# Attention scores by full-height matmuls over block-diagonally spread queries, four heads per matmul, in a fused adaLN + sliding-window attention + gMLP kernel

## The chip, the cores and the metric

The kernel runs on one core of a Trainium2 chip. The metric is the device time of one execution, in microseconds (us). The kernel before had a median of 351.53 us over three runs (351.22 to 391.38). All five engines of the core take part: TensorE (called PE in the profile, its weight loads PEld), VectorE (DVE), ScalarE (ACT), GpSimd (POOL) and SyncE (SP), which here only issues DMAs.

The clock that is granted to TensorE differs between runs of the same kernel, and every run reports its mean. In this study the kernel before ran in 343.8 to 346.9 us at a clock of 0.985, in 345.4 to 346.7 at 0.970, in 350 to 354 at 0.949 to 0.956, in about 356 at 0.937, once in 359 at 0.924, and in 388 to 392 at 0.816. The run report calls a run slow when it is over 1.5% above the fastest run of the same kernel and the same call, and "fast runs" below are the others.

## The reference, cut to what matters

```python
# S = 2048 tokens, D = 448, H = 16 heads of Dh = 28, window W = 256, Fh = 896
mod = silu(c) @ w_mod                     # six rows of D: sa, ca, ga, sb, cb, gb
h = layernorm(x) * (1 + ca) + sa
q, k, v = split_heads(h @ wqkv)
scores = (q @ k.T) * Dh ** -0.5           # key i visible to query t if 0 <= t - i < 256
x = x + ga * ((softmax(mask(scores)) @ v) @ wo)
h = layernorm(x) * (1 + cb) + sb
z = gelu(h @ w_in);  z1 = z[..., :Fh];  z2 = layernorm(z[..., Fh:])
g = w_sp @ z2 + b_sp                      # w_sp: 2048 x 2048, mixes tokens
x = x + gb * ((z1 * g) @ w_out)
```

The window makes every tile of 128 queries see at most three blocks of 128 keys: its own (masked above the diagonal), the one before (not masked), and the one before that (masked the other way).

## The kernel before: the parts that the change and the argument touch

The kernel is written as a list of operations with dependencies, priorities and estimated costs. A list scheduler in Python runs once, before compilation; it simulates the five engines with those costs and fixes **the order of the instructions on each engine**. On the chip each engine then executes its own list strictly in order and waits on semaphores. So an estimate in the source (the `1000` in `dma=(131072, 1000)` is the latency in ns that the scheduler assumes for a DMA) never slows the chip by itself; it decides where in an engine's list the consumer stands.

The queries and keys are stored transposed and padded: four heads of 32 rows in 128 partitions. A score matmul takes one head, hence 32 rows of the array, and 128 columns. One exp covers two heads and up to three key blocks (768 columns).

```python
# scores: one matmul per head and key block, 32 rows high
for bi in reversed(range(nb)):
    if on_pe and bi == nmask - 1:                  # last three tiles: mask by matmul
        for hi in range(2):
            mm(e, ps[:, ten.slot + hi, 0:nmask*128], ident[:], maskn[:, 256-nmask*128:256], True, False)
    for hi, h in enumerate(heads):
        hh = h % 4
        mm(e, ps[:, ten.slot + hi, bi*128:(bi+1)*128],
           QKT[32*hh:32*hh+32, 4 + hg, kb*128:(kb+1)*128],
           QKT[32*hh:32*hh+32, hg, j*128:(j+1)*128], ..., tile_position=(32*hh, 0))
# exp (ACT), masks of 128x256 (POOL, except in the last three tiles), P @ V: 29 columns per head (28 + a column of ones)
...
# projections: D = 448 in four chunks of rows; the fourth is only 64 rows high
KC = ((0, 128), (1, 128), (2, 128), (3, 64))
mm(e, ps[:, ten.slot, 0:w], WQK[0:kw, kc, 4*g:4*g+4, :], hT[0:kw, kc, c0:c1], kc == 0, kc == 3)
...
# a tile's attention output: transposed by DMA (SyncE), then multiplied with wo
t1 = P.op("oT%d" % j, pr, [("sp", 1260, lambda e: e.dma_start_transpose(out=oT[...], in_=o_sb[...]))],
          [nrm, t_opad], alloc=oTt, table="tr", dma=(131072, 1000), uses=[ot])
...
# the spatial weights: 32 transposing DMAs, also on SyncE, in the background of the attention
wsp_op[(si, hf)] = P.op(..., [("sp", 1300, fn)], deps, table="wsp", dma=(390000, 1500))
```

## Time and profile before

| stage (profile of 343.6 us) | from | to | length |
|---|---|---|---|
| start, up to the first projection matmul (`ps<-hT,WQK`) | 0 | 17.4 | 17.4 |
| projections and attention | 17.4 | 170.3 | 152.9 |
| MLP (from the first matmul on `hT` and `w_in_sb`) and last stores | 170.3 | 343.6 | 173.3 |

The profiled run took 345.4 us at a clock of 0.970, so the time is the span plus 1.8 us. The first three fences are the kernel before. From its page: the busy share of TensorE in 40 slices of 8.6 us (in tenths, 9 is 90% or more), the granted clock in the same slices, the chain of waits that ended last, and some groups of instructions (busy us in all, mean ns of one, then idle time before them and what ended it).

```profile
span 343.6 us, 6679 instructions
...
PE   0799999999999999999999999999999999999995
...
PEclk9999999999999999995589999999999999999999
...
PE 91%; DMA 2%; DVE 2%; POOL 2%; ACT 1%; issue 0%; DVEq 0%; ACTq 0%
...
L681 ACT ACTIVATE PT<-ps 128x768 bf16<-128x768 f32 (+2 forms) x128 | 96.7, 770 | 37.1 <-PE ps L453 33.4
...
L453 PE MATMUL ps<-QKT 32*128 32x128 bf16 x720 | 46.2, 225 | 1.0 <-ACT PT L681 0.9
...
L692 POOL TENSOR_SCALAR_AFFINE_SELECT PT<-PT 128x256 bf16<-128x256 bf16 x104 | 43.2, 416 | 7.0 <-ACT PT L681 6.8
...
L453 PE MATMUL ps<-wo_sb,oT 128*128 128x448 bf16 x64 | 21.9, 382 | 0.2 <-DMA oT<-o_sb 0.2
```

TensorE is the bound: it is on 91% of the chain and the score group waited 1.0 us in all. But "busy" does not say what it is busy with. Matmuls are pipelined and overlap in the records (the sum of busy times counts an overlap once per group), so a mean of 225 ns is not the cost of a matmul. The cost is the step from one end to the next. The timeline of TensorE gives ends as start plus length (columns: start, length, engine, line, operation, tile and form as rows*columns, count):

```profile
101.25 0.30 PE L453 MATMUL ps<-Vaug,PT 128*128 128x29 bf16 x6
101.40 0.35 PE L453 MATMUL ps<-wqkv_sb,hT 128*128 128x448 bf16 x1
101.68 0.34 PE L453 MATMUL ps<-QKT 32*128 32x128 bf16 x6
101.95 0.36 PE L453 MATMUL ps<-wqkv_sb,hT 64*128 64x448 bf16 x1
102.24 0.31 PE L453 MATMUL ps<-Vaug,PT 128*128 128x29 bf16 x6
102.41 0.35 PE L453 MATMUL ps<-wo_sb,oT 128*128 128x448 bf16 x1
102.69 0.34 PE L453 MATMUL ps<-QKT 32*128 32x128 bf16 x6
```

The ends are 101.55, 101.75, 102.02, 102.31, 102.55, 102.76, 103.03. Where the height stays at 128 rows, the 448-column matmul ends 0.20 or 0.21 us later. Where the height changes, everything costs about 0.1 us more: the 64-row 448-column matmul takes 0.29 us, the six score matmuls 0.27 us (over the trace their ends come in pairs of two row groups, about 54 ns from pair to pair; three such steps would be 0.16), and the six 29-column matmuls after a 64-row one 0.24 us (6 x 25 ns would be 0.15). Over the whole trace, a 512-column matmul ends 216 ns after its predecessor when both are 128 rows high, and 322 ns after a 32-row one. From 17.3 to 140 us I count 328 such changes. The elapsed 122.8 us are 86.6 us of streaming, 34.4 us for 328 changes at 105 ns, and 1.8 us of rest. (The rest is what remains when every change is counted at 105 ns, so it is an estimate.)

The 216 ns agree with the Trainium skill, "TensorE: Matmul & The Clock Gate", section "Wait — 56ns, not 53.3ns?", which measures, at full clock, N/2.4 GHz plus about 2.5 ns from one back-to-back matmul to the next, 215.7 ns for N = 512.

The table by windows shows the second loss. Columns: window, length, busy time and count of PE, PEld, DVE, ACT, POOL, granted clock, DMA share, GB/s:

```profile
150.00:160.00 10.00, 9.54 (x108) 4.56 (x104) 2.35 (x8) 5.83 (x8) 0.55 (x1) 0.67 0.52 107
160.00:170.00 10.00, 9.87 (x94) 4.07 (x92) 2.38 (x7) 5.07 (x7) 0.55 (x1) 0.50 0.14 26
```

In the last tiles of the attention, where masks are matmuls, the granted clock falls to 0.67 and 0.50.

### The profile page before, as it was taken

What the parts mean: (1) busy time and instruction counts of PE and PEld (TensorE: products, weight loads), DVE (VectorE), ACT (ScalarE), POOL (GpSimd) and SP (SyncE); (2) the same over time, 40 slices, a digit from 0 to 9 for tenths busy, and PEclk for the clock granted to TensorE, in tenths of its full rate; (3) what the DMA queues carried; (4) which work ended last, traced back from release to release, by engine and by line L of the source; (5) the groups of instructions that cost most, each with busy time, mean ns of one, the idle gap of its engine ahead of it and who ended that gap; (6) DMA issues with size and microseconds to landing.
All of it is one profiled execution on the core that took longest, in us unless ns stands there. A gap on an engine that the chain in (4) does not pass through costs nothing.

```text
span 343.6 us, 6679 instructions
## 1 busy us (share of the span) xinstructions
PE 327.6 (95%) x2728; PEld 160.0 (47%) x2728; DVE 172.8 (50%) x402; ACT 143.2 (42%) x198; POOL 100.9 (29%) x247
## 2 busy tenths in 40 slices
PE   0799999999999999999999999999999999999995
PEld 0524554445555555544444444444444444444442
DVE  1895468786566555332157787123243233233333
ACT  0347667678788777675555566600000000000000
POOL 5123447789878788100012212000000000000000
PEclk9999999999999999995589999999999999999999
DMA  6997488998212120673010000000010001001001
GB/s 194 333 359 181 99 126 164 142 162 148 46 34 33 34 48 19 128 150 62 17 31 15 2 2 0 2 0 0 2 53 0 2 0 53 2 0 53 2 0 53
DMA packets 60062, 23.64 MB, mean 69 GB/s; under 512 B 52224, under 2 KB 58560, under 8 KB 60032
## 3 DMA queue, kind: packets, MB, share of 16 engines
q1 hardware_dynamic: 59552, 23.21, 30.8%
q8 instruction: 22, 0.36, 0.4%
q10 hardware_dynamic: 480, 0.00, 0.1%
q14 instruction: 8, 0.07, 0.1%
HBM read 8.78 MB, written 1.84 MB: 31 GB/s over the span
## 4 chain that ended last, share of the span: by engine, by line
PE 91%; DMA 2%; DVE 2%; POOL 2%; ACT 1%; issue 0%; DVEq 0%; ACTq 0%
PE ps L453 91%; DMA cT_sb<-in_c_dram 2%; ACT PT L681 1%; POOL PT L692 1%; POOL rs_all L516 1%; POOL PT L690 1%; DVE WQK L576 0%; ACT L445 0%; DVE fin L864 0%; DVE st_all L520 0%; DVE hT L568 0%; ACT hT L564 0%; DVE Vaug L626 0%; DVE sc_rep L447 0%; DVEq L873 0%
## 5 line engine op out<-in xcount | busy, mean ns | idle before, releaser
L681 ACT ACTIVATE PT<-ps 128x768 bf16<-128x768 f32 (+2 forms) x128 | 96.7, 770 | 37.1 <-PE ps L453 33.4
L453 PE MATMUL ps<-w_spA,z_73 128*128 128x512 bf16 x336 | 77.1, 379 | 0.0
L842 DVE TENSOR_TENSOR tmpg<-ps,bsp_bc 128x512 bf16<-128x512 f32 x28 | 19.4, 692 | 72.1 <-PE ps L453 72.1
L453 PEld LDWEIGHTS ps<-w_spA,z_73 128*128 128x128 bf16 x336 | 32.9, 98 | 39.4
L516 POOL TENSOR_TENSOR rs_all<-ve_all,neghalf 128x1 f32<-128x1 f32 (+2 forms) x40 | 23.8, 601 | 87.7 <-DVE ve_all L514 87.7
L453 PE MATMUL ps<-QKT 32*128 32x128 bf16 x720 | 46.2, 225 | 1.0 <-ACT PT L681 0.9
L453 PE MATMUL ps<-hT,WQK 128*128 128x512 bf16 (+3 forms) x160 | 45.4, 341 | 0.1
L692 POOL TENSOR_SCALAR_AFFINE_SELECT PT<-PT 128x256 bf16<-128x256 bf16 x104 | 43.2, 416 | 7.0 <-ACT PT L681 6.8
L690 POOL TENSOR_SCALAR_AFFINE_SELECT PT<-PT 128x256 bf16<-128x256 bf16 x88 | 36.3, 413 | 20.1 <-ACT PT L681 18.5
L453 PEld LDWEIGHTS ps<-Vaug,PT 128*128 128x128 bf16 x720 | 29.4, 97 | 14.8 <-issue 5.6
L453 PE MATMUL ps<-Vaug,PT 128*128 128x29 bf16 x720 | 35.5, 178 | 0.1
L453 PEld LDWEIGHTS ps<-QKT 32*128 32x128 bf16 x720 | 21.0, 93 | 26.3 <-PE ps L453 13.8
L453 PE MATMUL ps<-w_spB,z_73 128*128 128x512 bf16 x112 | 28.7, 379 | 0.0
L453 PE MATMUL ps<-w_in_sb,hT 128*128 128x448 bf16 (+1 forms) x128 | 28.4, 366 | 0.0
L453 PE MATMUL ps<-hT,w_in_sb 128*128 128x512 bf16 x112 | 27.0, 380 | 0.0
L820 ACT ACTIVATE z1T<-ps 128x512 bf16<-128x512 f32 x28 | 16.6, 598 | 17.4 <-PE ps L453 17.4
L520 DVE BATCH_NORM_STATS2 st_all<-z2raw 128x6 f32<-128x448 bf16 x32 | 19.5, 622 | 8.2 <-ACT z2raw L800 8.2
L520 DVE BATCH_NORM_STATS2 st_all<-x_sb 128x6 f32<-128x448 bf16 x32 | 19.0, 609 | 6.1 <-DMA x_sb<-in_A_x_dram 5.8
L453 PE MATMUL ps<-wo_sb,oT 128*128 128x448 bf16 x64 | 21.9, 382 | 0.2 <-DMA oT<-o_sb 0.2
L453 PE MATMUL ps<-w_out_sb,z1T 128*128 128x448 bf16 x112 | 21.8, 352 | 0.0
L453 PEld LDWEIGHTS ps<-hT,WQK 128*128 128x128 bf16 (+1 forms) x160 | 13.3, 95 | 16.0 <-issue 7.1
L606 DVE CAST QKT<-ps 128x256 bf16<-128x256 f32 (+1 forms) x28 | 14.8, 534 | 11.3 <-PE ps L453 11.3
(67 smaller groups left out, 270.5 us busy)
## 6 DMA issues: line engine op xcount, KB each, us to landing
x_sb<-in_A_x_dram SPq DMA_DIRECT2D x4, 448.0 KB, 8.5
out_dram<-fin SPq DMA_DIRECT2D x16, 112.0 KB, 1.7
w_in_sb<-in_B_w_in_dram SPq DMA_DIRECT2D x1, 1344.0 KB, 11.6
wqkv_sb<-in_A_wqkv_dram SPq DMA_DIRECT2D x1, 1008.0 KB, 9.1
wmod_sb<-in_w_mod_dram SPq DMA_DIRECT2D x1, 1008.0 KB, 9.4
w_out_sb<-in_B_w_out_dram SPq DMA_DIRECT2D x1, 784.0 KB, 13.1
wmod_sb<-in_w_mod_dram SPq DMA_DIRECT2D x1, 672.0 KB, 6.9
bsp_bc<-in_B_b_sp_dram SPq DMA_DIRECT2D x1, 512.0 KB, 13.7
```

Source lines behind the costliest of these rows:

```text
L453: return e.matmul(out_, lhsT=lhsT, rhs=rhs, start=st, stop=sp, **kw)
L516: return P.op(name + "rs", prio, [("pool", 500 + 130 * (t1 - t0 - 1), lambda e: e.tensor_tensor(rs_all[:, slot, t0:t1], ve_all[:, slot, t0 ...
L520: st = [P.op("%sst%d" % (name, i), prio, [("dve", dve_ns(D, base=145), lambda e, i=i, s_=s_: e.bn_stats(st_all[:, slot, t, i, :], s_()))], ...
L606: return e.tensor_copy(QKT[:, g, c0:c1], ps[:, ten.slot, 0:w])
L681: return e.activation(ptv(pt)[:, :, 0:nb, :], ps[:, ten.slot:ten.slot + 2, 0:nb * 128].rearrange("p h (b q) -> p h b q", q=128), ACT.Exp, ...
L690: e.affine_select(out=v[:, :, 0, :], in_=v[:, :, 0, :], pattern=[[0, 2], [-1, 128]], compare_op=ALU.is_gt, fill=0.0, base=0, channel_multi ...
L692: return e.affine_select(out=v[:, :, nmask - 1, :], in_=v[:, :, nmask - 1, :], pattern=[[0, 2], [1, 128]], compare_op=ALU.is_ge, fill=0.0, ...
L820: z1_op[(ft, tb)] = P.op("z1g%d_%d" % (tb, ft), pr, [("act", act_ns(512), lambda e, tb=tb, ft=ft, ten=ten: e.activation(z1T[:, ft, tb * 51 ...
L842: a = P.op("ga%d_%d" % (tb, ft), pr, [("dve", 692, lambda e, tb=tb, ten=ten, tg=tg: e.tensor_tensor(tmpg[:, tg.slot, :], ps[:, ten.slot, : ...
```

## The change: its intent, and the diff

The intent is to keep the array at full height. Queries are spread block-diagonally: a buffer of 128 partitions x (4 heads x 128 queries) holds head hh only in its own 32 partitions and zeros elsewhere. One matmul of 128 rows and 512 columns then gives the scores of four heads at once, against the 128-row key tile. SyncE makes the spread by four DMAs per pair of tiles, into two buffers that one GpSimd memset has zeroed. An exp now covers 1024 columns, and GpSimd makes all masks, 512 columns each. The fourth chunk of the projections becomes 65 rows (the 65th is a bias row, because the modulation is now folded into the weights) and that of the output projection is padded to 128. From the second block on, layer-norm outputs are transposed by DMA instead of by matmul. The conditioning vector is loaded as a row. The last spatial weights go to a third buffer.

The diff holds more than this list: sixteen warm-up matmuls on the identity at the start, new pacing constants for the scheduler, another order of the score units, and a rule that lets the spatial-weight transposes out only from the fourth tile on, some 2.5 per tile.

```diff
-    QKT, qkt_off, qkt_end = alloc("QKT", [128, 8, S], BF16)
+    KT, kt_off, _ = alloc("KT", [128, 4, S], BF16)
+    NQB = 2
+    QB_sb, _, _ = alloc("QB_sb", [128, NQB, 4, 4, 256], BF16)
+    qst, _, q_end = alloc("qst", [128, 2, 4, 512], BF16)
...
+    t_qb0 = pool1("qb0", -59.4, 4000, lambda e: e.memset(QB_sb[:], 0.0))
...
+    qb_m, t_bq = bias_row("bq", -43.5, 0, wqkv_sb, 0, t_sA + t_wqkv, WQK[64:65, 3, 0:16, 0:DH])
...   # WQK and wqkv scaled by the modulation, on DVE, POOL or ACT
+                hT_op[t] = P.op("hT%d" % t, pr + 0.2, [("sp", 1260, lambda e, t=t, ten=ten: e.dma_start_transpose(
+                    out=hT[:, t, :, :], in_=xn[:, ten.slot, :]))], [xn_op[t], t_xpad], table="tr", dma=(131072, 1000), uses=[ten])
...
+                def fn(e, hh=hh, pair=pair, tb=tb, off=off):
+                    return e.dma_start(QB_sb[32 * hh:32 * hh + 32, qb_ten[pair].slot, :, hh, :],
+                                       qst[32 * hh:32 * hh + 32, qst_ten[tb].slot, :, off:off + 256])
+                qb_op[(pair, hh)] = P.op("qb%d_%d" % (pair, hh), j - 4, [("sp", 560, fn)], ..., dma=(65536, 1500), ...)
...
-                        last = mm(e, ps[:, ten.slot + hi, bi * 128:(bi + 1) * 128],
-                                  QKT[32 * hh:32 * hh + 32, 4 + hg, kb * 128:(kb + 1) * 128],
-                                  QKT[32 * hh:32 * hh + 32, hg, j * 128:(j + 1) * 128], ...,
-                                  tile_position=(32 * hh, 0))
+                for b, (hg, back) in enumerate(unit):
+                    kb = j - back
+                    last = mm(e, ps[:, ten.slot + b, :].rearrange("p (h q) -> p h q", h=4), KT[:, hg, kb * 128:(kb + 1) * 128],
+                              QB_sb[:, qb_ten[j // 2].slot, hg, :, (j % 2) * 128:(j % 2) * 128 + 128], True, True)
...
-                return mm(e, ps[:, wt.slot, 0:D], oT[0:kw, oTt.slot, kc, :], wo_sb[0:kw, kc, :], kc == 0, kc == 3)
+                return mm(e, ps[:, wt.slot, 0:D], oT[:, oTt.slot, kc, :], wo_sb[:, kc, :], kc == 0, kc == 3)
...
+    for o in late_loads:                       # MLP weights, second half of w_mod, b_sp: 4 MB
+        o.order += [hT_op[t] for t in QB[1]]   # issued only after these transposes
```

## The prediction

> **What bounds the kernel now.** TensorE. The page has it busy 327.6 of 343.6 us; the chain of waits runs 91% through the one matmul line. Matmul ends are modelled, so I took the steps between successive ends in the timeline. From 30 to 140 us TensorE never rests: about 76 of 110 us are streaming (216 ns per 512-column matmul, 25 per 29-column one, about 27 per 32-row score matmul, since two row groups run side by side), 2 idle, and 32 are spent where the height of the matmul changes. A 128-row 512-column matmul after a 32-row one ends 322 ns later rather than 216; a 32-row one after a 128-row one 157 rather than 53; a projection's 64-row fourth chunk pays too. That is about 105 ns per change, 302 changes here, about 411 (43 us) after 17 us. The Trainium skill, "TensorEngine Tiling (Array Packing)", Key Properties, says that changing the tiling mode drains the TensorE; the trace agrees. Besides, the granted clock falls to 0.50-0.8 from 153 to 175 us (table by windows), costing about 8 us.
>
> **What the change removes.** Scores become 180 full-height matmuls of 216 ns (39 us) for 720 in 128 units that now cost 20 us streaming and 27 us of changes: 8 us less, zeros included. The fourth chunk becomes 65 rows (bias row) or 128 (padded output weights). Together nearly all 43 us go and 19 come back. Masks by matmul for the last three tiles (48 x 107 ns, 5 us) and 48 transposes (3 us) leave TensorE. Dense scores should keep the clock full: 8 us. The conditioning vector, read as columns, lands at 7.7 us; as a row about 3. First projection about 14 us instead of 17.4.
>
> **What it adds.** The queries' DMAs, twelve DMA transposes (one lands in 2.4 to 4.7 us), bias rows, weight scaling. ACT: 90 exps of about 1.02 us (from 382/597/810 ns at 256/512/768 columns): 92 us for 96.7. GpSimd: masks of 512 columns, estimated 0.66 us from 413 ns at 256, eight per tile: 74 us, 110 in all. Per tile TensorE needs about 7.1 us with projections, ACT, GpSimd and DVE 6.2 each: less slack; in the last three tiles, without projections, ACT limits.
>
> **Sum.** TensorE needs about 115 us between the first projection and the MLP stage, 166 for the MLP (560 matmuls at 216 ns, 240 at 189, unchanged and gap-free now), 4 for the last store: 14 + 115 + 6 (exp-bound end) + 7 (waits, estimated) + 166 + 4 = 312 us of span. Times run about 7.5 us over the span. All the gain is in the first 170 us.
>
> **Predicted:** 319 us, 306 to 331. Faster by over 2%: 0.96; within: 0.03; slower: 0.01.
>
> **What would show it.** No height changes but in the bias rows; 512-column scores 216 ns apart; clock 1.00 after 15 us; exps of 1.02 us nearly back to back (ACT over 85% in attention); first exp at about 22 us; MLP from about 142 us, of equal length.
>
> **What would make it wrong.** GpSimd masks slower than estimated, or DVE and GpSimd slowing each other, making masks the bound; query DMAs or transposes queued behind the spatial-weight transposes, stalling TensorE; two score buffers only, so TensorE waits in order for each exp; a longer start through bias rows and scaling; the last spatial weights, loaded only after attention, arriving late.

## The result, and the profile after

The changed kernel had a median of 330.87 us (329.64 to 334.48, four runs). Beside it the kernel before had a median of 351.55. The ratio of the fast runs is 0.9432, with a 95% interval from 0.9336 to 0.9527. A ratio is the mean time of one kernel's fast runs over the mean of the other's fast runs of the same rounds, so it is not quite the ratio of the medians. The change is faster, but by less than predicted: the median lies at the upper edge of the range, 306 to 331.

The change was run once more beside the first experiments (label `e0_after`); its profile is used below where an experiment is compared with it.

| | before | predicted | after (first profile) | after (second, `e0_after`) |
|---|---|---|---|---|
| first projection at | 17.4 | 14 | 22.7 | 22.4 |
| first projection to MLP | 152.9 | 128 | 136.2 | 131.7 |
| MLP to the end | 173.3 | 170 | 173.8 | 173.0 |
| span | 343.6 | 312 | 332.7 | 327.1 |
| time minus span | 1.8 | 7.5 | 1.8 | 1.7 |

From the page of the changed kernel, the first profile, the same parts as before:

```profile
span 332.7 us, 5342 instructions
...
PE   6399996999999988886989999999999999999995
...
PEclk9589997899999999999999999999999999999999
...
PE ps L465 69%; DMA oT<-o_sb 7%; DMA QB_sb<-qst 3%; DVE xn L578 3%; ACT PT L741 3%; DVE st_all L556 2%; SPq L709 2%; POOL rs_all L552 1%; SPq L425 1%; PE ps L460 1%; SPq L584 1%; DVE mv_all L559 1%; DVE WQK L623 1%; POOL PT L752 0%; POOL PT L754 0%
...
L741 ACT ACTIVATE PT<-ps 128x1024 bf16<-128x1024 f32 x90 | 87.6, 1023 | 28.6 <-PE ps L465 28.0
...
L465 PE MATMUL ps<-QB_sb,KT 128*128 128x512 bf16 x180 | 52.5, 383 | 5.2 <-ACT PT L741 3.1
...
L752 POOL TENSOR_SCALAR_AFFINE_SELECT PT<-PT 128x512 bf16<-128x512 bf16 x56 | 35.6, 635 | 42.3 <-ACT PT L741 41.7
...
L465 PE MATMUL ps<-wo_sb,oT 128*128 128x448 bf16 x64 | 16.9, 379 | 8.9 <-DMA oT<-o_sb 8.1
```

The hollow of the clock at the end of the attention is gone (0.5 in the second slice and 0.7 in the seventh are new, and are taken up below). The chain has changed its character: TensorE's share falls to 69%, and DMAs and SyncE's queue appear in it. The exps and masks have the predicted lengths. The output projection now waits 8.1 us for its transposes; in the kernel before the same group waited 0.2 us (last line of the first fence).

The timeline of TensorE in the changed kernel answers the one shown before:

```profile
131.76 0.71 PE L465 MATMUL ps<-hT,WQK 128*128 128x256 bf16 x5
132.31 0.59 PE L465 MATMUL ps<-QB_sb,KT 128*128 128x512 bf16 x2
132.74 0.35 PE L465 MATMUL ps<-Vaug,PT 128*128 128x29 bf16 x8
132.94 0.49 PE L465 MATMUL ps<-hT,WQK 65*128 65x256 bf16 x3
133.27 0.35 PE L465 MATMUL ps<-Vaug,PT 128*128 128x29 bf16 x8
133.47 0.59 PE L465 MATMUL ps<-QB_sb,KT 128*128 128x512 bf16 x2
```

The ends are 132.47, 132.90, 133.09, 133.43, 133.62, 134.06: 0.215 and 0.22 us per score matmul, 24 ns per 29-column matmul, 113 ns per 256-column one. Nothing is paid between kinds, and a 65-row matmul among 128-row ones is free too. From 17 to 158 us I count 12 changes of height, all at bias rows. So the mechanism of the change works as intended. Of the 141 us elapsed there, 115.5 are streaming, 1.3 the changes, and 24 are waits. Before, the waits were 1.8 of 122.8. The gain was partly turned into waits, and the rest of this document is about which.

**The start.** Timeline of the first microseconds of the changed kernel:

```profile
7.31 0.36 DVE L578 TENSOR_SCALAR xn<-x_sb,mv_all,rs_all 128x448 bf16<-128x448 bf16 x1
...
7.66 7.79 DVE L578 TENSOR_SCALAR xn<-x_sb,mv_all,rs_all 128x448 bf16<-128x448 bf16 x3
8.39 6.92 POOL L446 MEMSET QB_sb<- 128x8192 bf16 x1
...
15.50 0.72 PE L465 MATMUL ps<-ident,xn 128*128 128x128 bf16 x5 [3.34 <-DVE xn L578]
```

A normalisation takes VectorE 0.36 us. The last of the first four takes 6.97 us, exactly while GpSimd zeroes the query buffer. The matmuls that transpose its result start at 15.50. Then come the modulation columns, two bias rows (19.2 to 21.1 us) and the scaling of the weights, and the first projection starts at 22.7. The clock of 0.5 falls in that slice, where TensorE is busy for three tenths; that the one caused the other is not shown here. The memset is not the whole of it: the projection weights, too, landed only at 14.6 us (12.1 in the kernel before), and the weights of the modulation at 10.0 (8.5 before).

**The second pair of tiles.** SyncE's timeline (SPq; a length here is the time SyncE spends issuing), and TensorE's at the same place:

```profile
33.63 0.59 SPq L412 DMA_DIRECT2D wmod_sb<-in_w_mod_dram  x1
...
36.14 3.83 SPq L425 DMA_DIRECT2D bsp_bc<-in_B_b_sp_dram  x1
40.01 3.33 SPq L709 DMA_DIRECT2D QB_sb<-qst  x4
43.39 8.70 SPq L584 DMA_TRANSPOSE hT<-xn  x4
52.13 2.57 SPq L778 DMA_TRANSPOSE oT<-o_sb  x2
```

```profile
49.69 0.38 PE L465 MATMUL ps<-hT,WQK 128*128 128x512 bf16 x1
52.09 1.02 PE L465 MATMUL ps<-QB_sb,KT 128*128 128x512 bf16 x4 [2.02 <-DMA QB_sb<-qst]
```

The 4 MB of late weights are issued from 33.6 to 40 us; the query copies of the second pair follow on the same queue and land only 8 to 10 us after their issue. Scores of the third tile start at 52.09, and ScalarE has no exp from about 41 to 52 us. TensorE itself had projections to do until 50.07; its own wait for these copies is 2.02 us.

**SyncE in the middle.** The changed kernel issues 140 DMAs from SyncE against 98 before: 32 query copies (0.60 us of issue each) and 12 transposes (1.26 us each) more, and two loads fewer. From 60 to 120 us SyncE is issuing for 55.8 of 60 us (57.1 in the second profile), against 34.6 before. Of the 22.5 us between the second profile and the kernel before, 9.6 are query copies, 5.5 transposes of layer-norm and attention outputs, and 7.3 spatial-weight transposes: these are no more in number than before, but 17 of the 32 now fall into this stretch instead of 11, since 14 of them were begun before 60 us in the old kernel and one in the new. From the end of a tile's attention output to the issue of its transpose it takes 3.1 us on average (2.9 in the second profile), against 0.26 before.

### The profile page after: what moved, and what is told of

Same layout as the page of the kernel before. It is cut to its first block, busy times and chain, and to the rows that moved or that the text cites. A ratio compares the mean times of both kernels' runs of the same rounds, so it can differ in the third digit from the quotient of the medians.

```text
span 332.7 us, 5342 instructions
## 1 busy us (share of the span) xinstructions
PE 303.9 (91%) x2109; PEld 151.6 (46%) x2120; DVE 174.2 (52%) x388; ACT 136.9 (41%) x164; POOL 109.0 (33%) x174
## 4 chain that ended last, share of the span: by engine, by line
PE 70%; DMA 9%; DVE 9%; SPq 4%; ACT 3%; POOL 2%; issue 2%; DVEq 0%; POOLq 0%
PE ps L465 69%; DMA oT<-o_sb 7%; DMA QB_sb<-qst 3%; DVE xn L578 3%; ACT PT L741 3%; DVE st_all L556 2%; SPq L709 2%; POOL rs_all L552 1%; SPq L425 1%; PE ps L460 1%; SPq L584 1%; DVE mv_all L559 1%; DVE WQK L623 1%; POOL PT L752 0%; POOL PT L754 0%
## 5 line engine op out<-in xcount | busy, mean ns | idle before, releaser
L741 ACT ACTIVATE PT<-ps 128x1024 bf16<-128x1024 f32 x90 | 87.6, 1023 | 28.6 <-PE ps L465 28.0
L465 PE MATMUL ps<-w_spA,z 128*128 128x512 bf16 x244 | 58.2, 379 | 0.4
L465 PE MATMUL ps<-QB_sb,KT 128*128 128x512 bf16 x180 | 52.5, 383 | 5.2 <-ACT PT L741 3.1
L752 POOL TENSOR_SCALAR_AFFINE_SELECT PT<-PT 128x512 bf16<-128x512 bf16 x56 | 35.6, 635 | 42.3 <-ACT PT L741 41.7
L552 POOL TENSOR_TENSOR rs_all<-ve_all,neghalf 128x1 f32<-128x1 f32 (+2 forms) x40 | 22.9, 575 | 47.9 <-DVE ve_all L550 47.8
L465 PE MATMUL ps<-hT,WQK 128*128 128x512 bf16 (+3 forms) x160 | 37.2, 338 | 1.1 <-DVE st_all L556 0.6
L465 PEld LDWEIGHTS ps<-w_spA,z 128*128 128x128 bf16 x252 | 24.6, 98 | 29.6
L754 POOL TENSOR_SCALAR_AFFINE_SELECT PT<-PT 128x512 bf16<-128x512 bf16 x56 | 36.7, 656 | 0.0
L465 PE MATMUL ps<-w_spB,z 128*128 128x512 bf16 x110 | 28.5, 379 | 0.1
L873 ACT ACTIVATE z1T<-ps 128x512 bf16<-128x512 f32 x28 | 16.6, 598 | 17.8 <-PE ps L465 17.8
L789 DVE TENSOR_TENSOR x_sb<-ps,x_sb 128x448 bf16<-128x448 f32 x16 | 9.9, 621 | 25.5 <-PE ps L465 25.3
L465 PE MATMUL ps<-w_spC,z 128*128 128x512 bf16 x83 | 22.7, 379 | 0.1
L465 PEld LDWEIGHTS ps<-QB_sb,KT 128*128 128x128 bf16 x180 | 14.1, 97 | 17.1 <-PE ps L465 7.4
L465 PEld LDWEIGHTS ps<-hT,WQK 128*128 128x128 bf16 (+1 forms) x160 | 14.6, 97 | 13.5 <-DVE st_all L556 1.0
```

The costliest lines, as they stand in the source:

```text
L465: return e.matmul(out_, lhsT=lhsT, rhs=rhs, start=st, stop=sp, **kw)
L552: return P.op(name + "rs", prio, [("pool", 500 + 130 * (t1 - t0 - 1), lambda e: e.tensor_tensor(rs_all[:, slot, t0:t1], ve_all[:, slot, t0 ...
L741: return e.activation(PT[:, pt.slot, :, :].rearrange("p (b h) q -> p b (h q)", b=2), ps[:, ten.slot:ten.slot + 2, :], ACT.Exp, scale=SCALE)
L752: e.affine_select(out=v[:, 0:4, :], in_=v[:, 0:4, :], pattern=[[0, 4], [-1, 128]], compare_op=ALU.is_gt, fill=0.0, base=0, channel_multipl ...
L754: return e.affine_select(out=v[:, 4:8, :], in_=v[:, 4:8, :], pattern=[[0, 4], [1, 128]], compare_op=ALU.is_ge, fill=0.0, base=0, channel_m ...
L789: x1_op[j] = P.op("x1_%d" % j, pr, [("dve", 624, lambda e, j=j, wt=wt: e.tensor_tensor(x_sb[:, j, :], ps[:, wt.slot, 0:D], x_sb[:, j, :], ...
```

## The experiments

All experiments that change the new kernel are edits of it; two are edits of the kernel before (`b1`, `b2`). Each ran three rounds (four runs with the profile); times are medians. The sets ran on four chips, and the changed kernel itself ran only in the first set, so differences between sets lean on fast runs having the same clocks. "Excess" of a group means: the steps between ends, less the streaming time, summed where the difference exceeds 60 ns, from 17 us to the first MLP matmul. Where the text says that the order of instructions was dealt anew, part of a difference can be the luck of that order.

### The control

No edit.

> The changed kernel again, unedited, as the control of this call: 329 to 335 us, span 328 to 333 us, first query/key projection at about 22.7 us, second-stage (MLP) matmuls from about 159 us. The other runs of this call are read against it.

Measured: 330.13 us (328.82 to 330.80, clocks 0.977 to 0.984). The kernel before in the same set had seven runs: two fast, 343.78 and 346.14 us, and five slow, 351.07 to 355.64. The ratio of the fast runs is 0.9565 (0.9487 to 0.9643); the run report's verdict on it is "unclear", with two fast runs of the kernel before. What follows: against fast runs of the kernel before the gain is 4.3%; the 5.7% of the first comparison contains a share of the lower clock of the old kernel's runs there.

### Theories

Theory 1 (start): the one large memset holds VectorE, and this is what delays the start and the end. Theory 2 (SyncE): its issue time is saturated, so that output transposes are late and TensorE waits for them in its fixed order. Theory 3 (late weights): their transfer holds up the second pair. The rivals: each of these is off the critical path, or the wait only moves.

### Split the memset

```diff
-    t_qb0 = pool1("qb0", -59.4, 4000, lambda e: e.memset(QB_sb[:], 0.0))
+    t_qb0 = 16 memsets e.memset(QB_sb[:, i, g, 2*k:2*k+2, :], 0.0) of 512 columns, one operation to the scheduler
```

> Same instruction order on every engine; the one GpSimd memset of the queries' buffer (128x8192, 6.92 us) becomes sixteen of 512 elements. Theory: a DVE normalisation (0.36 us by itself) that starts while one GpSimd memset runs is held until that instruction ends, so three of them took 7.79 us. Then the three take under 2.5 us, the first projection moves from 22.7 to about 18 us, and the kernel gains 3.5 to 5 us. Rival 1: the normalisations wait for something else of the memset's length, or GpSimd's traffic as a whole slows DVE: they still take about 7 us and nothing moves. Rival 2: weights and bias rows set the start (the projection weights land at 14.5 us): the normalisations shorten, but the first projection stays past 21 us.

Measured: 330.77 us, no gain. Its timeline:

```profile
7.47 0.36 DVE L585 TENSOR_SCALAR xn<-x_sb,mv_all,rs_all 128x448 bf16<-128x448 bf16 x1
...
7.81 1.39 DVE L585 TENSOR_SCALAR xn<-x_sb,mv_all,rs_all 128x448 bf16<-128x448 bf16 x3
8.55 7.66 POOL L451 MEMSET QB_sb<- 128x512 bf16 x16
```

The hold itself is shown: the last normalisation takes 0.57 instead of 6.97 us, while the memsets take 7.66 us in all. The Trainium skill, "SBUF — State Buffer", section "Who interferes with whom", says that VectorE in a two-port mode and GpSimd share a port pair under an exclusive lock which is held for a whole instruction. The trace agrees: VectorE stood for as long as the one 6.92 us memset and no longer than about one 0.5 us piece when it was split. (In which mode VectorE ran, the trace does not show.)

But the first projection only came from 22.4 to 21.1 us. GpSimd did not become free sooner, and two of the weight scalings stand behind the memset in its list (3.05 us for the two, from 17.9 us; TensorE waited 3.4 us for them). VectorE, in its fixed order, sat at a layer-norm statistic of the next block until 15.84 us because that x was still being loaded, with the modulation columns ready behind it. And the projections then waited 7.1 us in excess instead of 1.7. The MLP began at 156.0 us, against 154.1 in the control. The start has several chains of nearly equal length; removing the longest one gave 1.3 us.

### Relieve SyncE: plain copies in place of the spatial-weight transposes

```diff
-    e.dma_start_transpose(out=w_spT(si)[:, hf*1024:(hf+1)*1024], in_=B_w_sp[hf*1024:(hf+1)*1024, si*128:(si+1)*128])
+    e.dma_start(w_spT(si)[:, hf*1024:(hf+1)*1024], B_w_sp[si*128:(si+1)*128, hf*1024:(hf+1)*1024])
```

The result is wrong (the spatial weights are not transposed). The order on every engine is the same, so this is the cleanest of the tests.

> Wrong results on purpose: the 32 spatial-weight transposes become plain copies of the same bytes into the same places; instruction order of PE, ACT, DVE and GpSimd unchanged. Theory: SyncE's sequencer is the new limit in the middle (it issues DMAs for 18 to 19 of 20 us from 60 to 120 us, 1.3 us per transpose), so the output transposes are issued late and TensorE waits for them. Then the issues shrink to about 0.6 us, the waits of TensorE for the output transposes (12 us with those of the weight loads) fall under 4 us, and the kernel gains 5 to 9 us. Rival: the two score buffers and the in-order exps pace TensorE: under 1.5 us gained.

Measured: 324.82 us (323.88 to 326.34), 5.3 us less than the control of the same set. An issue takes 0.43 to 0.54 us instead of 1.30, SyncE is issuing for 44.3 of 60 us instead of 57.1, the excess at the output projection falls from 7.4 to 3.7 us, and first projection to MLP from 131.7 to 127.3 us. The list of waits (columns: who waits, for what, us in all, times, longest), first the control, then this kernel:

```profile
ACT PT L741 <- PE ps L465: 23.8, 28, 2.9
...
PE ps L465 <- DMA oT<-o_sb: 4.6, 4, 1.9
```

```profile
ACT PT L741 <- PE ps L465: 19.6, 27, 2.9
...
PE ps L465 <- DMA oT<-o_sb: 1.7, 2, 1.3
```

TensorE waits 1.7 us for output transposes instead of 4.6, and ScalarE, which gets its scores from TensorE, waits 4.2 us less. A rival is that the transposes loaded the DMA engines, and not SyncE. The kept traces speak against it: from issue to landing an output transpose took 2.73 us on average in the control and 2.72 here; what shrank is the time from its input to its issue, 2.9 to 2.2 us. What follows: SyncE's issue time was on the critical path, mostly through the output projection, and cost about 5 us, 4.1 of them before the MLP. The Trainium skill, "DMA: Bandwidth & Descriptors", section "Issuing engines are not separate DMA queues", calls the time that it takes to initiate a DMA "usually small relative to the DMA itself". Here the issue of one transpose took 1.3 us against about 4 us to its landing, and 140 issues made it a bound.

### Let the query copies of the second pair overtake the late weights

```diff
+    # after scheduling: on SyncE, the four copies of pair 1 moved to directly behind those of pair 0
+    P.order[at:at] = [o for o in P.order if o.name.startswith("qb1_")]
```

> Only SyncE's order changes: the four query copies of the second tile pair go right behind those of the first, ahead of the weights loaded late (4 MB). Theory: these copies, issued at 40 us and landing 8 to 10 us later, kept TensorE and ACT waiting until 52 us and halved the granted clock to 59 us. Then the exps of tile 2 start by about 46 us, no idle time over 1 us ends at 52 us, the clock stays 1.00 after 25 us, and 3 to 6 us are gained. Rival: TensorE had other work until 50 us anyway, and the transposes of the normalised input behind the same loads hold the next tiles: under 1.5 us gained.

Measured: 331.81 us, 1.7 us more than the control. The wait moved, as the rival had it: the layer-norm transposes that feed the projections now stood behind the weights (the excess at the projections 5.2 us instead of 1.7), the exps of the second tile started at 41.7 us instead of 37.2, those of the third at 54.5 instead of 51.8. What follows: what has to be brought in before 52 us is much for that stretch (in the control the DMA share, which can exceed 1 in this view, is 1.04 from 40 to 45 us and 1.49 from 45 to 50), and here the order within the queue only chose who waited.

### Later output projections in TensorE's list

If the wait for SyncE costs time only because the output projection stands too early in TensorE's list, it is enough to tell the scheduler that this transpose takes longer.

```diff
-    [nrm, t_opad], alloc=oTt, table="tr", dma=(131072, 1000), uses=[ot])      # the oT transposes only
+    [nrm, t_opad], alloc=oTt, table="tr", dma=(131072, 3000), uses=[ot])
```

> The changed kernel planned with 2 us more latency for the output transpose, so TensorE meets the output projection later; this reshuffles the static order somewhat. Theory (SyncE issues late, the plan is too hopeful): TensorE's waits for these transposes (4.6 us, 7.4 us of excess time in the first stage in the control) fall under 2 us and 2 to 5 us are gained. Rival: the waiting moves to the scores (exp pace) and under 1.5 us are gained.

Measured: 325.79 us (324.59 to 326.27), 4.3 us less than the control (of another set, at the same clocks, 0.977 to 0.984). SyncE is as busy as before, 55.8 of 60 us, and the output transposes are issued as late as before, 3.2 us after their input; but the excess at the output projection is 1.6 us instead of 7.4. From its list of waits:

```profile
ACT PT L741 <- PE ps L465: 19.4, 30, 3.3
...
PE ps L465 <- DMA oT<-o_sb: 1.6, 3, 0.8
```

What follows: nearly all that a fast SyncE would give back is had without making SyncE any faster. The cost arose from a 1 us assumption in a static order, where issue delay and landing took about 6 us.

### Fewer, larger transposes

```diff
-    for hf in range(2):  ...  dma_start_transpose(out=w_spT(si)[:, hf*1024:...], in_=B_w_sp[hf*1024:..., ...])
+    for hf in range(1):  ...  dma_start_transpose(out=w_spT(si), in_=B_w_sp[:, si*128:(si+1)*128])   # all 2048 rows
```

> The changed kernel with 16 spatial-weight transposes of 2048 rows instead of 32 of 1024: same bytes, same transposing. If SyncE's issue time is the cost (1.3 us whatever the size), its busy time in the middle falls by about 20 us and 3 to 6 us are gained, as in the run with plain copies (5.3). If instead the transposes' load on the DMA engines delays the output transposes, or the issue time grows with the size, under 1.5 us are gained.

Measured: 330.32 us, no gain. An issue now takes 1.93 to 2.38 us (medians of the three buffers) instead of 1.30, so halving the count saved little: SyncE is issuing for 54.7 of 60 us. Issue time grew with the transpose, so this run could not part SyncE from the DMA engines; the landing times above do.

### A shorter start

Split memset, no weight scaling on GpSimd, and VectorE's statistics of the second block behind the modulation columns.

```diff
+    16 memsets, as above
-    ("pool", 650, lambda e, d=dst, s_=src, sc=sc: e.tensor_scalar(d, s_, sc, None, ALU.mult)),   # one of three choices for the scaling
+    for o in statistics of block 1: o.order += t_sA + t_cA
```

> Split memset as before, and besides: the statistics of the second block of x wait for the modulation columns (in the split run DVE sat in them from 13 to 15.8 us for data while these columns were ready), and the weight scaling doesn't use GpSimd (3.05 us there for two). Theory: with these three gone only the landing of the projection weights (14.5 us), a bias row and the scaling are left: first projection at 17.5 to 18.5 us, 3 to 4 us earlier than the control's 22.4. If the start is on the critical path as the prediction had it, the kernel gains 2 to 4 us; if later waits (second pair's query copies behind the late weights, landing at 51 us) take the gain back, the second-stage matmuls start as in the control (154 us) and under 1 us is gained.

Measured: 334.81 us (333.56 to 335.45), 4.7 us more than the control. The start itself did what it should: the first projection came at 18.8 us instead of 22.4, the scores at 29.5 instead of 33.2. But by the third tile only 1.1 us were left of the 3.6 (50.7 against 51.8), the query copies still standing behind the late weights; and in the new order the excess at the output projection was 13.0 us (the longest 3.1 us), against 7.4 in the control. What follows: nothing yet about the worth of the start. A repair that changes the inputs of a static scheduler also deals a new order, and here the new order cost more than the repair gained.

### Late weights not held back

```diff
-    for o in late_loads:
-        o.order += [hT_op[t] for t in QB[1]]
```

> The changed kernel without the rule that the 4 MB of late weights wait for the second block's transposes: they go out at 12 to 16 us, as in the kernel before, when the DMA engines are at 20% from 20 to 30 us. Theory: in the control the exps of tile 2 start at 51.8 us whatever happens before (also 3.6 us earlier a start left them at 50.7), because the second pair's query copies land behind these weights. Then tile 2 starts by 45 us and the kernel gains 3 to 7 us. Rival: TensorE needs the time to 50 us for the second block's projections anyway, so tile 2 starts a few us earlier and later tiles as before: under 2 us.

Measured: 332.03 us (327.98 to 334.38, one run slow); the three fast runs, 327.98 to 332.36, lie around the control. The third tile's exps start at 47.9 us instead of 51.8, but the first tile's at 41.9 instead of 34.5, and from the fourth tile on nothing is won (58.6 against 59.6, then 70.2 against 68.4). The rival's number was right, but not for its reason: the weights now stood in the way of the first tile (DMA share 1.05 to 1.33 from 20 to 40 us).

### Late weights issued from ScalarE

```diff
+    for o in late_loads: o.opts = [("act", o.opts[0][1], o.opts[0][2])]
```

> The same rule kept, but the late weights are issued from ACT's queue instead of SyncE's (about 3 to 6 us of ACT's time once). If the query copies and transposes are late because they queue behind the weights on SyncE's queue, they now land in under 5 us instead of 8 to 10 and tile 2 starts by about 47 us: gain 2 to 5 us. If they are late because the DMA engines are full (share over 1.1 from 40 to 50 us), they stay late and ACT's blocked time costs: no gain or a loss of up to 3 us.

Measured: 338.97 us, 8.8 us more. With the weights issued from ScalarE without regard to SyncE's queue, layer-norm transposes took up to 17.8 us and query copies up to 13.4 us from issue to landing; the first exps started at 40.6 us, those of the third tile at 60.9. ScalarE spent 6.7 us issuing them, and the order was dealt anew. What follows: leaving SyncE's queue did not help, and the late landings fit DMA engines that are full in this stretch (DMA share 1.15 from 34 to 40 us, 1.27 from 50 to 55). This agrees with the same section of "DMA: Bandwidth & Descriptors" as above, by which all issuers share the same 16 DMA engines.

### Query copies issued from ScalarE

```diff
-    P.op("qb%d_%d" % (pair, hh), j - 4, [("sp", 560, fn)], ...)
+    P.op("qb%d_%d" % (pair, hh), j - 4, [("act", 600, fn)], ...)
```

> The 32 query copies (0.6 us of issue each, 20 us) move from SyncE's queue to ACT's; nothing else. Theory (SyncE's issue time is the limit in the middle): its busy time from 60 to 120 us falls from 57 to under 50, outputs wait less before their transposes are issued (2.9 us mean in the control, 0.3 in the kernel before). As ACT pays 20 us, of which it has slack until about 125 us and none in the last tiles: gain of 0 to 4 us. If SyncE isn't the limit: a loss of 2 to 6 us, ACT's issue time added to its exps.

Measured: 335.33 us, 5.2 us more. SyncE is relieved (42.0 of 60 us) and output transposes are issued 1.0 us after their input, but ScalarE now pays 22.4 us of issue time: the excess at the scores is 11.0 us instead of 7.6, and the MLP begins at 160.6 us. The excess at the output projection did not fall with SyncE's load; it rose, 9.5 us instead of 7.4, in an order dealt anew. So a relieved SyncE alone does not end that wait; where the output projection stands in TensorE's list counts as much. The Trainium skill, "Perfetto Trace Analysis", section "DMA Optimizations", says that where descriptor generation is the bottleneck, balancing over the engines that can issue "may help". Here it did not: ScalarE had 13.9 us idle from 60 to 120 us in the control, but its exps pace the last tiles (six exps per tile, see below).

### Before, with the fourth chunk at full height

One part of the change alone, in the kernel before: the fourth chunk of the projections padded with zeros to 128 rows. TensorE's order is unchanged.

```diff
+    four DVE memsets of rows 64:128 of chunk 3 of WQK, wqkv_sb, wo_sb and hT
-    ... WQK[0:kw, kc, ...], hT[0:kw, kc, c0:c1] ...      # also for V and for wo
+    ... WQK[:, kc, ...], hT[:, kc, c0:c1] ...
```

> The kernel before with one part of the change alone: the 64-row fourth chunk of the query/key, value and output projections is padded with zeros to 128 rows (same matmuls, same order on TensorE, four small memsets more). Scores stay at 32 rows. Theory: each change of matmul height costs TensorE about 105 ns and TensorE has no idle time; the changes fall from about 411 to about 305, so 8 to 11 us are gained (about 341 to 344 us). Rival: the fourth chunk costs what it does for another reason (its weight load can't hide, or ACT paces the stage): under 3 us.

Measured: 339.50 us at clock 0.963, 346.46 at 0.945, 340.20 at 0.964 and 332.44 at 0.999; the kernel before in the same set: 346.93 at 0.985, 346.11 at 0.970, and five slow runs from 351.37 to 391.57. Only the last of the four runs counts as fast, so there is no interval; the profile is of the first, a slow one. The changes of height from 17.3 to 140 us fell from 328 to 251. Runs at near clocks (339.5 and 340.2 at 0.963 and 0.964 against 346.1 at 0.970) differ by about 6 us, and 77 changes at 105 ns would be 8.1 us. The traces allow a comparison without the state of the clock: up to 130 us it was 1.00 in both. From the first projection to the exps of the thirteenth tile, the same work in the same order, the old kernel took 112.2 us and this one 106.3, 5.9 us less with 82 changes fewer (8.6 us at 105 ns); from 30 to 130 us TensorE was idle for 2.1 us instead of 0.6. What follows: the cost of the changes is shown by an experiment, and part of what is saved comes back as waits. For the whole run the state of the clock varies too much to give a number. The new scores alone were not isolated.

### Before, without masks by matmul

```diff
     def pe_mask(j, ui):
-        return j >= 13
+        return False          # GpSimd masks the last three tiles too
```

> The kernel before with the masks of its last three tiles on GpSimd like all others, instead of by matmul: 48 matmuls of 256 columns (5 us) and 48 changes of height (5 us) less on TensorE. Theory: TensorE bounds this stage, so up to 10 us are gained, unless the clock, which fell at 153 us, falls earlier because TensorE is less dense: the prediction's claim that 32-row scores without dense work let it fall would show as a mean clock under 0.9 from 140 to 165 us, and the gain as 3 to 7 us. Rival: the masks by matmul were there because GpSimd can't keep up: a loss.

Measured: 345.26 us; ratio of fast runs 1.0008 (0.9939 to 1.0077): no difference (the run report's verdict is "unclear", with two fast runs of the kernel before). Windows of the kernel before, then of this one:

```profile
140.00:160.00 20.00, 19.09 (x238) 9.69 (x238) 6.32 (x17) 12.54 (x16) 1.10 (x2) 0.83 0.64 133
160.00:180.00 20.00, 19.87 (x146) 8.73 (x145) 7.58 (x22) 10.67 (x15) 2.19 (x4) 0.65 0.14 27
```

```profile
140.00:160.00 20.00, 15.74 (x235) 8.68 (x233) 6.33 (x18) 12.95 (x17) 14.65 (x39) 0.71 0.75 127
160.00:180.00 20.00, 17.05 (x159) 8.13 (x161) 10.43 (x26) 11.21 (x15) 8.04 (x20) 0.70 0.20 41
```

TensorE lost 6.2 us of busy time in these 40 us and gained none of it, because it waited instead and because the clock was low in both windows. Taking the masks by matmul away did not keep the clock up. The first half of the expectation (a clock under 0.9, here 0.71) came out, the gain did not; whether the clock falls because the old scores are not dense was not tested. In the changed kernel the clock was 1.00 there in the first profile and 0.89 from 140 to 155 us in the second; what sets it was not settled.

### The shorter start and the later output projections together

```diff
+    the three edits of the shorter start, and dma=(131072, 3000) for oT
```

> Earlier start (split memset, no GpSimd scaling, statistics after the modulation columns) plus the output projection planned 2 us later. Theory A: first projection at 18.8 us, output-projection waits under 4 us, MLP matmuls from about 148 us, time 321 to 324 us. Theory B (the start is off the critical path): 325 to 327 us, as with the later output projection alone (325.8).

Measured: 322.80 us (322.72 to 324.74, clocks 0.979 to 0.995), ratio to the kernel before 0.9314 (0.9249 to 0.9380). This is the best kernel: 2.2% below the control by the medians, 3.0 us below the later output projections alone (of another set) and 2.1 below the run with 5000 ns of the same set. At near clocks the difference is 1.5 us (324.74 at 0.979 against 326.27 at 0.977) to 3.2 us (322.73 at 0.987 against 325.91 at 0.983). First projection at 18.8, MLP from 147.4, span 320.9. What follows: with the waits at the output projection out of the way (3.8 us of excess are left) an earlier start reaches the end: the first projection and the MLP both begin 4.0 us earlier than with the later output projections alone, and 1.5 to 3.2 us of it show in the time. It is one order; how much of it is the luck of that order was not tested.

### Ungated weights and the later output projections together

```diff
-    for o in late_loads: o.order += [hT_op[t] for t in QB[1]]
+    dma=(131072, 3000) for oT
```

> Late weights sent early, plus the output projection planned 2 us later. Theory A: exps of tile 2 at 48 us instead of 53 and the waits gone: 322 to 325 us. Theory B: 325 to 327 us.

Measured: 325.38 us (324.81 to 326.04), against 325.79 for the later output projections alone. Letting the late weights go early makes no difference here that is clear of the order.

### All three

```diff
+    shorter start, ungated weights, dma=(131072, 3000) for oT
```

> Earlier start, late weights sent early and the output projection planned 2 us later, all three. Theory A: gains add: MLP matmuls from about 145 us, 318 to 322 us. Theory B: 325 to 327 us.

Measured: 328.19 us (325.06 to 330.11, one run slow); the fast runs alone have a median of 327.81, worse than the best by 5.0 us. In the profile (of the slow run, at a clock of 0.979) the first scores start only at 42.1 us, and the excess at the scores is 14.1 us instead of 8.2, 8.4 of it in one wait. The repairs are not additive. That the ungated weights fill the stretch which the shorter start needs is the likely reason.

### A longer assumption still

```diff
-    dma=(131072, 1000)      # oT
+    dma=(131072, 5000)
```

> The changed kernel with the output projection planned 4 us later and nothing else. If the waits for the transposes were the cost, there is little left to gain over 2 us later: 323 to 327 us, waits under 1 us. If it is rather the luck of a static order, this one may lie anywhere from 323 to 333 us, with the waits under 1 us all the same.

Measured: 324.90 us (323.21 to 325.83), excess at the output projection 1.7 us. 3000 and 5000 give the same within about 1 us, two different orders of instructions. So the 4 to 5 us of the later output projections are not the luck of one order.

## Why the prediction was right or wrong, point by point

**Right: the mechanism.** "No height changes but in the bias rows": 12 from 17 to 158 us, against 328 from 17 to 140. "512-column scores 216 ns apart": 215 to 220. "About 115 us" of TensorE work between the first projection and the MLP: 115.5 us of streaming from 17 to 158, 113.0 between just these two points. The skill's page "TensorEngine Tiling (Array Packing)", section "Key Properties", says that a change of the tiling mode drains the TensorE; the traces agree in so far as each change costs about 105 ns. They do not show the drain itself. 65 rows between 128-row matmuls cost nothing.

**Right: sizes of single operations.** Exps of 1.02 us: 1023 ns, 87.6 us in all. Masks on GpSimd estimated at 0.66 us: 635 and 656 ns. An MLP of equal length: 173.0 to 173.8 us against 173.3. The end of the attention bound by exps, 6 us: from 120 us on the second profile advances by 6.0 to 6.5 us per tile, which is six exps, and its excess at the scores is 7.6 us.

**Failed steps.** The mechanism was right; two terms of the sum were not: the first, a start of 14 us, which measured 22.7 and 22.4, and the 7 us of waits in the middle. The next two points take them in turn.

**Mis-sized: the waits of the middle.** First projection to MLP was predicted as 128 us and measured 136.2 and 131.7. With SyncE relieved it was 127.3, with later output projections 128.5. The prediction allowed 6 us for the exp-bound end and 7 for waits, 13 in all. Measured between the same two points are 113.0 us of streaming in both profiles, 0.8 for eight changes of height, and waits of 22.4 us in the first profile and 17.9 in the second. The step that failed is the list of DMAs that were costed by landing time only: "twelve DMA transposes (one lands in 2.4 to 4.7 us)". What limited was SyncE's issue time, 0.6 us per query copy and 1.26 us per transpose, on a queue that was already busy for 34.6 of 60 us and on which more of the spatial-weight transposes were now put into the same stretch; and a scheduler that took 1 us for an output transpose where about 6 passed. The prediction did name "query DMAs or transposes queued behind the spatial-weight transposes, stalling TensorE" as what could make it wrong. For the output transposes that is what happened; the number it needed stood in the profile of before.

**Wrong: the start.** "First projection about 14 us instead of 17.4": it came at 22.7 and 22.4. This is the largest mis-sized term, 8.4 us of the 15.1 by which the second profile's span exceeds the predicted one (3.7 more are the middle, 3.0 the end). The step took the earlier conditioning vector (7.7 to 3 us) as the critical one. In fact the chain ran over a normalisation held for 6.6 us by the memset of the query buffer, then bias rows and weight scalings that had to be finished before the first projection. The prediction listed bias rows and scaling under "What it adds", but gave them no time. 14 us were out of reach in any case: the projection weights landed at 14.6 us, and even with the hold and its two neighbours removed the first projection came at 18.8, later than the old kernel's 17.4. "First exp at about 22 us" became 34.7. Removing the hold alone gave 1.3 us at the start and nothing at the end; removing it with two neighbours gave 3.6 us, which showed at the end only in the run where the output projection waited less.

**Wrong: "clock 1.00 after 15 us" and "ACT over 85% in attention".** The clock was below 1.00 in two windows of the first profile, 0.54 from 10 to 20 us and 0.67 from 50 to 60 us, the windows in which TensorE waited for the start and for the second pair. ScalarE was busy 45.5 of 60 us (76%) from 60 to 120 us: TensorE's waits came between.

**Wrong: "TensorE needs ... 166 for the MLP, 4 for the last store".** The last tile's output projection and transposes lie between the last scores and the last store as well; both kernels take 173 us from the first MLP matmul on.

**Wrong, in the other direction: "Times run about 7.5 us over the span".** Time minus span is 1.7 to 1.8 us in all runs of both kernels. The 7.9 us between the median and the profile's span are 1.8 us and a difference in clock: the profiled run took 345.4 us at 0.970, the median run was one of those near 351 us that later sets saw at 0.949 to 0.956. This error hid 5.8 us of the others: 312 + 15.1 + 1.7 is 328.8, the time of the second profiled run. It also means that part of the 5.7% of the first comparison, about 1.3 points by the control, is the state of the old kernel's clock and not the change. The prediction also hoped for 8 us from the clock at the end of the attention ("Dense scores should keep the clock full"). The clock there did rise, to 1.00 and 0.89, and the changed kernel's runs are steadier; but no run tests density, and taking the masks by matmul away did not keep the clock up. If the 8 us are in the gain, their reason is not shown.

**Open.** How much of the 21.2 us that the middle shrank by (152.9 to 131.7) belongs to the scores and how much to the fourth chunk; what decides the clock state of the old kernel; and why just the order of the shorter-start kernel had the longest waits at the output projection, although its output transposes were issued only 1.9 us after their input (2.9 in the control).

## What to carry to other kernels

When a change adds DMAs, cost the time their issue takes on the issuing engine as well as their landing, and read from the profile before how much of that engine's time is left in the stretch. In a statically ordered kernel an optimistic latency in the scheduler turns into a wait on the bottleneck engine: give late inputs a generous one before making them earlier, and test a repair again once the waits that can swallow it are gone. Check that the profiled run and the median run had the same granted clock before taking anything from the difference of the two.

## What the Trainium skill lacked or had wrong

- "TensorEngine Tiling (Array Packing)", Key Properties, names the drain on a change of mode but no cost. The runs show about 105 ns per change between 32, 64 and 128 rows, 34.4 of 122.8 us here, and none between 65 and 128 rows.
- "DMA: Bandwidth & Descriptors", "Issuing engines are not separate DMA queues": issue time is called usually small relative to the DMA. Here a transpose of 1024 rows was issued in 1.30 us, one of 2048 rows in 1.93 to 2.38 us, a 128-row one in 1.26 us, and a query copy in 0.60 us; SyncE spent 57.1 of 60 us issuing, and 12.8 us less of it went with 5.3 us less of the whole.
- "Perfetto Trace Analysis", "DMA Optimizations": balancing issues over the engines "may help"; here moving 32 copies to ScalarE cost 5.2 us, and ScalarE issued for 22.4 us.
- "SBUF — State Buffer", "Who interferes with whom": the trace fits it. What it does not give is a size for this case: a VectorE normalisation of 0.36 us took 6.97 us beside one 6.92 us GpSimd memset and 0.57 us beside the same memset in 16 pieces, which took 7.66 us in all.
- No page that I found, "TensorE: Matmul & The Clock Gate" with its cases of a clock that falls again included, says why the clock can be granted at 0.50 for ten microseconds while the profile has TensorE busy for 9.87 of them, nor why the same kernel runs at mean clocks from 0.816 to 0.985.
